# Two attention and two spectral layers on one core: later sums of squares, later squares, and wo products ahead of the filler

## The chip, the cores and the metric

The kernel runs on one core of one Trainium2 chip, in one launch. The metric is the time of an execution on the device, in microseconds (us). The kernel before took 3763.46 us, the median of three runs (3761.44 to 3765.95).

## The reference

An activation x of 2048 rows (S) and 1024 columns (D) goes through two equal pairs of sub-layers, each with a layer norm in front and a residual sum behind:

```python
def _A_ref(x, wqkv, wo):                       # 32 heads, Dh = 32
    qkv = (x @ wqkv).reshape(B, S, 3, H, Dh).transpose(2, 0, 3, 1, 4)
    q, k, v = qkv[0], qkv[1], qkv[2]
    scores = einsum("bhqd,bhkd->bhqk", q, k) * (Dh ** -0.5)
    p = softmax(scores, axis=-1)
    o = einsum("bhqk,bhkd->bhqd", p, v)
    return o.transpose(0, 2, 1, 3).reshape(B, S, D) @ wo

def _B_ref(x, w_r, w_i):
    X = rfft2(x, axes=(-2, -1)) * (w_r + 1j * w_i)
    return irfft2(X, s=(S, D), axes=(-2, -1))

x = x + _A_ref(_layernorm(x), wqkv, wo)
x = x + _B_ref(_layernorm(x), w_r, w_i)
x = x + _A_ref(_layernorm(x), wqkv, wo)
x = x + _B_ref(_layernorm(x), w_r, w_i)
```

All is float32 in and out. The change touches the attention sub-layers alone.

## The kernel before

**Units and groups.** `attention()` is called once per layer. It works through 8 head groups g of 4 heads; a group has 4 chunks c of 512 queries times 16 tiles kt of 128 keys, so 64 units. A unit computes the scores of one key tile against one query chunk for the 4 heads: `S` issues 12 matmuls (L697: high and low float16 halves of keys and queries, three products per head) into two PSUM buffers of the pool `psS`, and ScalarE takes one exponential per buffer (L701), 128 x 1024 each, with a bias that keeps it small. Every second unit `PV` multiplies the exponentials of two units by the values (L707, 16 matmuls in rows of the trace). VectorE adds the exponentials of a chunk up in `add`: two first sums L718 and then 28 additions L720 per chunk, two for a unit. When a chunk is over, `fin` runs at the start of the next one: the denominators z (L727, four products of a matrix of ones with the two sums, again in a `psS` buffer), a transposition L728, a reciprocal and more, and `out` follows at kt == 5.

`psS` has three buffers (`psS.tile` in `S`, `norms`, `wo_rest` and `fin`), taken in turn in the order of the code: two for a unit's scores, and whichever is next for the others. A user of a buffer waits for the one three turns before.

**Slots and the filler.** The keys, queries and values of later groups are projected in between. Every odd unit is a slot, 32 in a group, and in a slot `next(sl)` runs as many steps of the generator `filler` as the planner `slots` gives it. `qk_chunk` makes one chunk of 512 columns of keys or queries with 24 matmuls (L420) in one PSUM bank (`bank()`, the name x), then splits it in two halves (`split`, L215 on ScalarE and L216 on VectorE), then squares the high half (L427 on VectorE, or L425 on ScalarE in group 7's phases, which run in group 6), as `sq`. `v_tiles` does the same for values (L465). After a phase's fourth chunk the phase goes on the list `left_norms`.

**Sums of squares.** The exponential's bias of a group comes from the largest norms of its keys and queries. `norms` takes a `psS` buffer, sums the squares over each head's 32 rows with four small matmuls (L440, with the constant `bones`), and VectorE takes the maximum (L442, `mqk`); for queries `mkbias` follows on GpSimd. `slots` runs `norms` at the front of the first slot that it enters with the list not empty:

```python
while left_norms:
    norms()
```

In even groups the phases are the next group's keys and queries and the keys of the one after; in odd groups the next group's queries and values. The keys of the group after next, finished at the end of an even group, are summed in slot 0 of the odd one, and the queries of the next group in slot 12 of the odd one.

**Groups 6 and 7.** Group 6 projects the last keys and queries, chunk by chunk in turn, in 22 slots; then its slots multiply by wo. In group 7 each slot runs `share[u // 2]` steps of `wof`, which computes the tiles of the output projection up to the seventh of eight groups (`wo_part`, L526 and the evacuation L552), and in 11 slots (`rests`) a `wo_rest(t)`, which adds the last group's part: six matmuls in a `psS` buffer, an evacuation L567 with the residual on VectorE, two `bn_stats` (L569), a store `yd` and a `bn_aggr` (L588), for the next layer norm. The first four rests stand in slots 11, 12, 14 and 15, the last of them in the slot ahead of the end of chunk 1.

**Order.** TensorE and ScalarE run in the order in which the code issues (`tc.manual_schedule`). VectorE's instructions are ordered by the framework's scheduler. GpSimd and SyncE (which issues the DMAs) are not held by hand either.

Of the kernel before, what the change touches and what calls it, by code (L numbers as in the profile page):

```python
# [107 lines left out]
NG, NCH, NKT, NST = 8, 4, 16, 6  # L108
# [104 lines left out]
def split(nc, hi, lo, src, scale):  # L213

    high = nc.scalar.activation(hi, src, AF.Copy, scale=scale)  # L215
    return high, nc.vector.scalar_tensor_tensor(lo, src, scale, hi, op0=ALU.mult, op1=ALU.subtract)  # L216


def run(g):
    for _ in g:  # L220
        pass
# [115 lines left out]
def attention(nc, tc, layer, ap, xin, yd, wts, wo, cst, dram, flags):  # L337
# [14 lines left out]
    def bank():  # L352

        if both:
            both.append(True)
            if len(both) % 2:
                return psO.tile([128, 512], F32, name="o")
        return psX.tile([128, 512], F32, name="x")
# [48 lines left out]
    def qk_chunk(ph, c):  # L407
        kind, g = ph
        w = W[ph]
        if c == 0:  # L410
            if kind == "k":
                K[g] = ap.k[g % 3]
            else:
                Q[g] = qp.tile([128, 2, 2048], F16, name="Q") if g % 2 else ap.q
            p_, n_ = (qp, "Q") if ph == ("q", 0) else (wvp, "wv") if ph == ("q", NG - 1) else (sq, "sq")
            nrm[ph] = p_.tile([128, 4, 512], BF16, name="sq", tag=n_)
        t = (K if kind == "k" else Q)[g][:, :, c * 512:c * 512 + 512]
        ps = bank()
        for i, (a, b) in enumerate([(w[:, n, d], x[c][:, d]) for x, n in ((xh, 0), (xh, 1), (xl, 0)) for d in range(8)]):
            nc.tensor.matmul(ps, a, b, start=i == 0, stop=i == 23)  # L420
            if i < 23:
                yield
        split(nc, t[:, 0], t[:, 1], ps, SQ / (SX * SW))
        if g == NG - 1:
            nc.scalar.activation(nrm[ph][:, c], t[:, 0], AF.Square)  # L425
        else:
            (nc.gpsimd if both else nc.vector).tensor_tensor(nrm[ph][:, c], t[:, 0], t[:, 0], op=ALU.mult)  # L427
        if c == 3:
            left_norms.append(ph)
        yield  # L430

    left_norms = []

    def norms():
        kind, g = ph = left_norms.pop(0)
        if g not in mx:
            mx[g] = sm.tile([128, 2], F32, name="mqk")
        ps = psS.tile([128, 2, 512], F32, name="s")
        for c in range(4):
            nc.tensor.matmul(ps[32 * c:32 * c + 32, 0], cst["bones"], nrm[ph][:, c], start=True, stop=True)  # L440
        i = 0 if kind == "k" else 1
        nc.vector.reduce_max(mx[g][:, i:i + 1], ps[:, 0], axis=AX.X)  # L442
        if kind == "q":
            mkbias(g)
# [32 lines left out]
    def sums(ph):  # L477
        return 8 if ph[0] == "v" else 4
# [82 lines left out]
    def wo_last(c, t, p, src, y, start):  # L561

        for n in range(2):
            run(wo_mm(p[:, n], c, t, n, (7,), start=start))
        st = sm.tile([128, 2, 6], F32, name="st")
        r0 = c * 512 + t * 128
        nc.vector.scalar_tensor_tensor(y, p.rearrange("p n c -> p (n c)"), 1.0 / (SO * SW), src, op0=ALU.mult, op1=ALU.add)  # L567
        for n in range(2):
            nc.vector.bn_stats(st[:, n], y[:, n * 512:n * 512 + 512])  # L569
        nc.sync.dma_start(yd[r0:r0 + 128, :], y)  # L570
        return st
# [14 lines left out]
    def wo_rest(t):  # L586
        p = psS.tile([128, 2, 512], F32, name="s")
        nc.vector.bn_aggr(mvs[:, 2 * t:2 * t + 2], wo_last(t // 4, t % 4, p, wo_dst[t], wo_dst[t], True))  # L588
# [102 lines left out]
    def S(g, c, kt):  # L691

        s = [psS.tile([128, 2, 512], F32, name="s") for _ in range(2)]
        for i, (a, b) in enumerate(((0, 0), (0, 1), (1, 0))):
            for h in range(4):
                r = slice(32 * h, 32 * h + 32)
                nc.tensor.matmul(s[h // 2][:, h % 2], K[g][r, a, kt * 128:kt * 128 + 128],  # L697
                                 Q[g][r, b, c * 512:c * 512 + 512], start=i == 0, stop=i == 2)
        for hf in range(2):
            p = P[g, c, kt, hf] = pp.tile([128, 2, 512], F32, name="p")  # L700
            nc.scalar.activation(p, s[hf], AF.Exp, bias=bias[g], scale=SCALE / (SQ * SQ))  # L701

    def PV(g, c, kt):
        if kt == 0:
            O[g, c] = psO.tile([128, 512], F32, name="o")
        for h in range(4):
            nc.tensor.matmul(O[g, c][32 * h:32 * h + 32], V[g][:, kt, 32 * h:32 * h + 32], P[g, c, kt, h // 2][:, h % 2],  # L707
                             start=kt == 0, stop=kt == NKT - 1)
        if kt == NKT - 1:
            o = ap.oc.tile([128, 512], F32, name="oc")  # L710
            nc.scalar.copy(o, O[g, c])
            O[g, c] = o

    def add(g, c, kt):
        for hf in range(2):
            p = P[g, c, kt, hf]
            if kt == 1:
                nc.vector.scalar_tensor_tensor(acc[hf], P[g, c, 0, hf], 1e-34, p, op0=ALU.add, op1=ALU.add)  # L718
            elif kt:
                last_add = nc.vector.tensor_add(acc[hf], acc[hf], p)  # L720
        return last_add if kt > 1 else None
# [15 lines left out]
    def out(g, c, eng=nc.vector):  # L737
        r = O.pop((g, c))
        t = on2.tile([128, 2, 512], F16, name="ohl")
        nc.scalar.copy(t[:, 0], r)  # L740
        eng.tensor_tensor(t[:, 1], r, t[:, 0], op=ALU.subtract)
        if g < NG - 1:
            nc.sync.dma_start(od[:, g, :, c * 512:(c + 1) * 512].rearrange("a p n -> p a n"), t)
        else:
            olast[c] = t
# [3 lines left out]
    left, rests = 16, {}  # L749
# [4 lines left out]
    def slots(f, sums, n, steps):  # L754

        while sums:
            k = max(1, int(n / sums + 0.5))
            m = -(-steps // k)
            for i in range(0, steps, m):
                while left_norms:  # L760
                    norms()
                for _ in range(min(m, steps - i)):
                    next(f, None)
                n -= 1
                yield sums - (i + m >= steps)
            sums -= 1

    with tc.manual_schedule(engines={mybir.EngineType.PE, mybir.EngineType.Activation}):
        for g in range(NG):
            todo = sum(sums(ph) for ph in beside.get(g, []))  # L770
            sl = slots(fill, todo, 22 if g == NG - 2 else 32, 24)
            wsl = slots(wof, 4, 10, 21)
            for u in range(NCH * NKT):
                c, kt = divmod(u, NKT)
                S(g, c, kt)
                if g == u == 0:
                    run(last_v)
                if kt % 2 == 0:
                    for w in pend:
                        PV(*w)  # L780
                    late = pend
                    pend = []
                    if kt == 0 and late:
                        for w in late:
                            last_add = add(*w)
                        with tc.issue_after(last_add.ins):
                            wts.look()
                        done = [late[1][:2]]
                        fin(*done[0])
                        late = []  # L790
                for w in late[:1]:
                    add(*w)
                late = late[1:]
                if kt == 5 and done:
                    out(*done.pop())
                pend.append((g, c, kt))
                if kt % 2 == 0:
                    continue
                if todo:
                    todo = next(sl)  # L800
                elif g == NG - 2:
                    if left:
                        run(lwo)
                        left = 0
                    if next(wsl, None) is not None and u == NCH * NKT - 1:
                        run(wsl)
                elif g == NG - 1:
                    for _ in range(share[u // 2]):
                        next(wof)
                    if u // 2 in rests:  # L810
                        wo_rest(rests[u // 2])
                if g == NG - 2 and todo <= 6 and left > (8 if todo > 4 else 0):
                    next(lwo)
                    left -= 1
        for w in pend:
            PV(*w)
        for w in late + pend:
            add(*w)
        run(wof)
# [561 lines left out]
```

## Time and profile before

| | |
|---|---|
| median of three runs | 3763.46 us (3761.44 to 3765.95) |
| profiled execution, its own time | 3764.43 us |
| its span in the trace | 3762.6 us |
| mean granted TensorE clock | 0.996 |
| HBM read, written | 132.35 MB, 48.23 MB |
| the costliest groups: exponentials L701 on ScalarE | 2170.0 us in 2048 |
| additions L720 on VectorE | 2088.6 us in 1792 |
| PV matmuls L707 on TensorE | 985.0 us in 8192 |

The profiled execution is a single one, and 1.8 us of its time lie outside the span. In rows of the timeline the first number is the start in microseconds from the span's beginning, the second the time to the end of the last instruction of the row; `x12` says how many instructions the row holds, and a bracket at its end how long the engine waited before the row and for what. Rows of the waits give the engine and tile that waits, its line, whom it waits for with tile and line, and then total microseconds, how often, and the longest.

### The profile page before, as it was taken

The page shows a single profiled execution, that of the slowest core. Times are in us where ns is not written, and L with a number is a line of the kernel's source. Part 1 is how long each engine was busy: PE and PEld are TensorE (multiplying, and loading weights), DVE is VectorE, ACT ScalarE, POOL GpSimd, SP SyncE. Part 2 cuts the span into 40 slices and gives each one's busy share as a digit, 9 for nine tenths or more (in the row PEclk, how much of TensorE's full clock was granted, in tenths as well). Part 3 has the DMA queues.
Part 4 walks back from the last instruction along what each step waited for, and adds up shares of the span by engine and source line. Part 5 has one row for each costly group of instructions (what it writes and reads, how often), then busy time and mean ns, then how long its engine had stood idle before and what let it go on. Part 6 is the DMA issues. An engine that isn't in the chain of part 4 may idle for free.

```text
span 3762.6 us, 80259 instructions
## 1 busy us (share of the span) xinstructions
PE 3695.4 (98%) x33271; PEld 1637.1 (44%) x33271; DVE 3218.8 (86%) x3874; ACT 2900.2 (77%) x3587; POOL 298.8 (8%) x388
## 2 busy tenths in 40 slices
PE   8999999999999999999999999999999999999998
PEld 5333433343343333378963334333433433333788
DVE  7899899989999988975658998999899999789755
ACT  5788888888888866658748888888888888666686
POOL 1000000000000000014410000000000000000243
PEclk9999999999999999999999999999999999999999
DMA  6000000000000211233250000101000102111423
GB/s 194 10 18 18 13 13 17 26 7 18 13 27 15 88 54 65 74 143 106 70 157 21 29 29 24 32 24 35 14 29 29 41 15 85 54 71 68 166 86 109
DMA packets 150119, 198.43 MB, mean 53 GB/s; under 512 B 58224, under 2 KB 104048, under 8 KB 148720
## 3 DMA queue, kind: packets, MB, share of 16 engines
q1 hardware_dynamic: 148416, 192.62, 15.8%
q8 instruction: 263, 4.31, 0.5%
q14 instruction: 112, 0.92, 0.1%
q10 hardware_dynamic: 1328, 0.59, 0.1%
HBM read 132.35 MB, written 48.23 MB: 48 GB/s over the span
## 4 chain that ended last, share of the span: by engine, by line


## 5 line engine op out<-in xcount | busy, mean ns | idle before, releaser
L701 ACT ACTIVATE p<-s,bias 128x1024 f32<-128x1024 f32 x2048 | 2170.0, 1112 | 563.0 <-PE s L697 545.6
L720 DVE TENSOR_TENSOR R<-R,p 128x1024 f32<-128x1024 f32 x1792 | 2088.6, 1220 | 131.2 <-ACT p L701 126.8
L707 PE MATMUL o<-p,R 128*32 128x512 f32 x8192 | 985.0, 598 | 0.0
L420 PE MATMUL x<-big,wqk 128*128 128x512 f16 x2880 | 676.5, 380 | 2.3 <-ACT R L469 1.9
L697 PEld LDWEIGHTS <-R 32*128 32x128 f16 x12288 | 230.9, 92 | 749.2 <-issue 633.5
L420 PEld LDWEIGHTS <-wqk 128*128 128x128 f16 x3072 | 275.6, 98 | 418.4 <-issue 129.3
L707 PEld LDWEIGHTS o<-p,R 128*32 128x32 f32 x8192 | 213.6, 109 | 523.4 <-issue 523.4
L697 PE MATMUL s<-Q,R 32*128 32x512 f16 x6144 | 427.3, 377 | 4.6 <-DVE R L567 2.7
L697 PE MATMUL s<-R 32*128 32x512 f16 x6144 | 430.4, 377 | 1.5 <-ACT p L701 0.3
L465 PE MATMUL x<-wv,big 128*128 128x256 f16 x2784 | 330.6, 275 | 4.1 <-DVE R L216 2.2
L465 PEld LDWEIGHTS <-big 128*128 128x128 f16 x3072 | 290.9, 98 | 100.2 <-issue 59.3
L526 PE MATMUL x<-big 128*128 128x512 f16 x1050 | 241.6, 380 | 0.0
L448 POOL PARTITION_ALL_REDUCE mall<-mqk x16 | 38.4, 2401 | 2278.1 <-DVE mqk L442 2266.7
L526 PEld LDWEIGHTS <-big 128*128 128x128 f16 x1344 | 124.3, 98 | 176.4 <-issue 38.6
L718 DVE SCALAR_TENSOR_TENSOR R<-p 128x1024 f32<-128x1024 f32 x128 | 150.8, 1218 | 31.8 <-ACT p L701 31.8
L1043 DVE TENSOR_TENSOR H<-G,H 128x512 f16<-128x512 f32 (+1 forms) x68 | 47.0, 692 | 119.8 <-ACT H L1042 119.6
L988 ACT COPY U<-ps 64x256 f32<-64x256 f32 (+1 forms) x272 | 97.2, 357 | 9.2 <-PE ps L995 3.9
L988 ACT COPY B<-ps 64x256 f32<-64x256 f32 (+1 forms) x272 | 97.2, 357 | 5.4 <-PE ps L995 1.7
L995 PE MATMUL ps<-cbi,H 128*128 128x256 f16 (+1 forms) x792 | 98.6, 273 | 1.5 <-DVE H L1043 1.0
L728 DVE STREAM_TRANSPOSE zt<-s 128x512 f32<-128x512 f32 x64 | 45.8, 715 | 62.6 <-PE s L727 62.5
L995 PE MATMUL ps<-cb,big 128*128 128x256 f16 x780 | 96.7, 273 | 0.0
L995 PEld LDWEIGHTS <-H 128*128 128x128 f16 (+1 forms) x792 | 76.5, 98 | 12.4 <-DVE H L1043 2.4
(443 smaller groups left out, 2981.7 us busy)
## 6 DMA issues: line engine op xcount, KB each, us to landing
wst<-in_wp SPq DMA_DIRECT2D x96, 256.0 KB, 3.0
R<-y SPq DMA_DIRECT2D x32, 512.0 KB, 5.2
w<-in_w SPq DMA_DIRECT2D x60, 256.0 KB, 2.7
od<-ohl SPq DMA_DIRECT2D x56, 256.0 KB, 2.4
big<-od SPq DMA_DIRECT2D x16, 896.0 KB, 5.9
y<-R SPq DMA_DIRECT2D x20, 512.0 KB, 2.6
wst<-in_wo SPq DMA_DIRECT2D x32, 256.0 KB, 2.7
xres<-in_x SPq DMA_DIRECT2D x16, 512.0 KB, 3.6
```

Of the source, the lines that this page charges most:

```text
L420: nc.tensor.matmul(ps, a, b, start=i == 0, stop=i == 23)
L465: nc.tensor.matmul(ps[:, j], x[c][:, d, o:o + 128], w[:, n, d], start=i == 0, stop=i == 23)
L526: nc.tensor.matmul(p, a, b, start=start and d == ds[0] and i == 0, stop=stop and d == ds[-1] and i == 2)
L697: nc.tensor.matmul(s[h // 2][:, h % 2], K[g][r, a, kt * 128:kt * 128 + 128], Q[g][r, b, c * 512:c * 512 + 512], start=i == 0, stop=i == 2)
L701: nc.scalar.activation(p, s[hf], AF.Exp, bias=bias[g], scale=SCALE / (SQ * SQ))
L707: nc.tensor.matmul(O[g, c][32 * h:32 * h + 32], V[g][:, kt, 32 * h:32 * h + 32], P[g, c, kt, h // 2][:, h % 2], start=kt == 0, stop=kt == ...
L718: nc.vector.scalar_tensor_tensor(acc[hf], P[g, c, 0, hf], 1e-34, p, op0=ALU.add, op1=ALU.add)
L720: last_add = nc.vector.tensor_add(acc[hf], acc[hf], p)
L728: nc.vector.transpose(zt.rearrange("p a b -> p (a b)"), z)
L988: nc.scalar.copy(ov[64 * r:64 * r + 64, a0:a0 + m, x], tl[64 * x:64 * x + 64, :m, r])
L995: nc.tensor.matmul(out, l, r, start=k == 0, stop=k == len(mm_) - 1)
L1043: nc.vector.tensor_sub(lo, gs, hi)
```

## The change

Three orders change; the instructions and their sizes stay as they are.

1. **Sums of squares.** A phase that ends is put in a set `fresh` too. `slots` calls `ripe()` before it runs `norms`: in even groups below 6 it says yes as before; in odd groups and in group 6 it says no once for a phase just ended, and yes in the next slot. So `norms` of the keys in odd groups moves from slot 0 to slot 1, that of the queries from slot 12 to slot 13, and in group 6 both last ones a slot later (20 to 21, 22 to 23).
2. **Squares on ScalarE in group 6.** For the first three of four chunks of each of the last two phases, `qk_chunk` yields before the square, so it is issued at the first filler step of the next slot, behind the exponentials of the two units between. These are 6 of 8 squares per layer.
3. **Last head group.** In a slot of group 7 `wo_rest` now runs ahead of the slot's `wof` steps.

```diff
@@ qk_chunk
         split(nc, t[:, 0], t[:, 1], ps, SQ / (SX * SW))
         if g == NG - 1:
+            if c < 3:
+                yield
             nc.scalar.activation(nrm[ph][:, c], t[:, 0], AF.Square)
+            if c < 3:
+                return
         else:
             (nc.gpsimd if both else nc.vector).tensor_tensor(nrm[ph][:, c], t[:, 0], t[:, 0], op=ALU.mult)
         if c == 3:
             left_norms.append(ph)
+            fresh.add(ph)
         yield
 
-    left_norms = []
+    left_norms, fresh = [], set()
+
+    def ripe():
+        if not left_norms:
+            return False
+        old = left_norms[0] not in fresh or (g % 2 == 0 and g < NG - 2)
+        fresh.clear()
+        return old
@@ slots
-                while left_norms:
+                while ripe():
                     norms()
@@ the unit loop, group 7
                 elif g == NG - 1:
+                    if u // 2 in rests:
+                        wo_rest(rests[u // 2])
                     for _ in range(share[u // 2]):
                         next(wof)
-                    if u // 2 in rests:
-                        wo_rest(rests[u // 2])
```

In the changed code every line from 432 on is 12 further down (L442 is L454, L697 is L709, L720 is L732, and so on); the squares L425 and L427 become L427 and L431.

The order of the instructions on VectorE and ScalarE, before and now, at three places. The first is on VectorE in group 1 of layer 0, around the maximum of the queries (`mqk<-s`). Before:

```order
L216 SCALAR_TENSOR_TENSOR R<-x,R 128x512
L427 TENSOR_TENSOR sq<-R 128x512
L720 TENSOR_TENSOR R<-R,p 128x1024 x2
L442 TENSOR_REDUCE mqk<-s 128x1
L720 TENSOR_TENSOR R<-R,p 128x1024 x14
```

Now, the same place:

```order
L216 SCALAR_TENSOR_TENSOR R<-x,R 128x512
L431 TENSOR_TENSOR sq<-R 128x512
L732 TENSOR_TENSOR R<-R,p 128x1024 x6
L454 TENSOR_REDUCE mqk<-s 128x1
L732 TENSOR_TENSOR R<-R,p 128x1024 x10
```

The maximum stands behind six additions in place of two. The keys' maximum in odd groups likewise moves behind two first sums and two additions.

The second is on ScalarE in group 6 of layer 0, around the first square of a chunk of the last queries (`sq<-Q`; `big<-wst` are halves of wo, prepared in the same slots). Before:

```order
L215 ACTIVATE Q<-x 128x512
L425 ACTIVATE sq<-Q 128x512
L215 ACTIVATE big<-wst 128x512
L701 ACTIVATE p<-s,bias 128x1024 x4
L215 ACTIVATE big<-wst 128x512
L701 ACTIVATE p<-s,bias 128x1024 x4
```

Now, the same place:

```order
L215 ACTIVATE Q<-x 128x512
L215 ACTIVATE big<-wst 128x512
L713 ACTIVATE p<-s,bias 128x1024 x4
L427 ACTIVATE sq<-Q 128x512
L215 ACTIVATE big<-wst 128x512
L713 ACTIVATE p<-s,bias 128x1024 x4
```

The square stands behind the four exponentials of the next two units.

The third is on VectorE in group 7 of layer 0, from the last rest of chunk 1 (slot 15) to the denominators' first transposition (`zt<-s`). Before:

```order
L720 TENSOR_TENSOR R<-R,p 128x1024 x3
L552 SCALAR_TENSOR_TENSOR R<-x,xres 128x512
L720 TENSOR_TENSOR R<-R,p 128x1024
L567 SCALAR_TENSOR_TENSOR R<-s,R 128x1024
L569 BN_STATS st<-R 128x6 x2
L588 BN_AGGR mvs<-st 128x2
L728 STREAM_TRANSPOSE zt<-s 128x512
```

Now, the same place:

```order
L732 TENSOR_TENSOR R<-R,p 128x1024 x3
L579 SCALAR_TENSOR_TENSOR R<-s,R 128x1024
L564 SCALAR_TENSOR_TENSOR R<-x,xres 128x512
L581 BN_STATS st<-R 128x6 x2
L732 TENSOR_TENSOR R<-R,p 128x1024
L600 BN_AGGR mvs<-st 128x2
L740 STREAM_TRANSPOSE zt<-s 128x512
```

The chunk's last addition stood ahead of the rest's evacuation and its statistics, and stands behind them now. Only one store `yd` per layer moves by a place on SyncE (in slot 29), and GpSimd's order is the same.

## The prediction

> **What bounds the kernel now.** The page first, then TensorE's waits, then the timeline around each wait that the change touches.
>
> ```profile
> span 3762.6 us, 80259 instructions
> PE 3695.4 (98%) x33271; PEld 1637.1 (44%) x33271; DVE 3218.8 (86%) x3874; ACT 2900.2 (77%) x3587; POOL 298.8 (8%) x388
> ```
>
> TensorE is in work for 98% of the span. A change that leaves its matmuls as they are can only win its waits, or lose by new ones. The five rows of TensorE's waits that this change can touch (microseconds in total, times, longest):
>
> ```profile
> PE s L727 <- DVE R L567: 2.9, 2, 1.4
> PE s L697 <- DVE R L567: 2.7, 4, 0.9
> PE s L440 <- DVE sq L427: 2.4, 6, 0.4
> PE s L697 <- DVE mqk L442: 1.9, 6, 0.3
> PE s L440 <- ACT p L701: 0.4, 2, 0.2
> ```
>
> They sum to 10.3 us, 0.27% of the span. What is really lost is more, since a wait shorter than the pipe of matmuls shows as a longer group and not as idle time. So each place is measured from start to start, against the same stretch where nobody waits. About 0.2% (7.5 us) is what a measurement of this kernel can tell from no change.
>
> **Sums of squares, query of the next group (three odd groups, two layers: 6 times).** The timeline of group 1 in layer 0:
>
> ```profile
> 349.70 0.68 DVE L216 SCALAR_TENSOR_TENSOR R<-x,R 128x512 f16<-128x512 f32 x1
> 349.98 0.40 PE L440 MATMUL s<-sq,bones 128*32 128x512 bf16 x3
> 350.77 0.38 PE L440 MATMUL s<-sq,bones 128*32 128x512 bf16 x1 [0.40 <-DVE sq L427]
> 351.08 1.92 PE L465 MATMUL x<-wv,big 128*128 128x256 f16 x16
> 352.91 0.68 DVE L442 TENSOR_REDUCE mqk<-s 128x1 f32<-128x512 f32 x1
> 353.65 0.82 PE L697 MATMUL s<-Q,R 32*128 32x512 f16 x10 [0.32 <-DVE mqk L442]
> 354.40 1.92 PE L707 MATMUL o<-p,R 128*32 128x512 f32 x16
> ...
> 357.01 1.92 PE L465 MATMUL x<-wv,big 128*128 128x256 f16 x16
> ...
> 358.87 0.82 PE L697 MATMUL s<-Q,R 32*128 32x512 f16 x12
> 359.62 1.92 PE L707 MATMUL o<-p,R 128*32 128x512 f32 x16
> ```
>
> The reader sees two waits on VectorE: for the fourth quarter of the squares, and, at the next scores, for the maximum that frees the sums' PSUM buffer. Undisturbed paces from the last four rows: value products to scores 1.86 (357.01 to 358.87), scores to PV 0.75, PV to the next filler 2.61 (354.40 to 357.01). The other place, the key's sums at the front of an odd group, gives the sums' own length:
>
> ```profile
> 284.92 0.83 PE L697 MATMUL s<-Q,R 32*128 32x512 f16 x12
> 285.82 0.40 PE L440 MATMUL s<-sq,bones 128*32 128x512 bf16 x4
> 286.16 1.90 PE L420 MATMUL x<-big,wqk 128*128 128x512 f16 x8
> 287.61 0.68 DVE L442 TENSOR_REDUCE mqk<-s 128x1 f32<-128x512 f32 x1
> 287.99 1.18 PE L697 MATMUL s<-Q,R 32*128 32x512 f16 x12
> 289.10 1.92 PE L707 MATMUL o<-p,R 128*32 128x512 f32 x16
> ```
>
> That is 0.34 (285.82 to 286.16). So from 349.98 to the PV at 354.40 the query's place took 4.42 where 0.34 + 1.86 + 0.75 = 2.95 would do: 1.47 us lost.
>
> With the sums one slot later all of it does not come back, and the rows say why. The sums now hide the value products' own wait: their bank is free only when L216 ends, 349.70 + 0.68 = 350.38, so without the sums they start at 350.4 instead of 349.98. Then scores 352.3, PV 353.0, sums 355.65, value products 356.0, scores 357.85. The maximum now stands behind six additions of VectorE instead of two (the order given above), at the 1.13 of one addition (rows 1476.78 and 1477.91 below): 352.91 + 4 x 1.13 = 357.43. Before, the scores went on 0.74 after the maximum's start (352.91 to 353.65), so now at 358.17, a wait of 0.3, and their PV at 358.92 against 359.62. **Gain 0.70 each, 4.2 us in six.** It may be half an addition (0.57) better or worse each time, since VectorE's queue alone decides it: 0.8 to 7.6.
>
> **Sums of squares, key (6 times).** Lost before: 285.82 - 284.92 - 0.75 = 0.15, and 289.10 - 287.99 - 0.75 = 0.36, together 0.51. After: filler at 285.67, scores 287.50 (1.83 as from 286.16 to 287.99), PV 288.25, sums 290.86, filler 291.2, scores 293.03. The maximum moves behind two first sums and two additions: 287.61 + 4 x 1.13 = 292.13, and it frees its buffer at 292.87, just in time. **Gain 0.51 each, 3.1 us**; at least 0, at most that. The per-group bias that both maxima feed is wanted at the next group's first exponential, tens of microseconds on.
>
> **Squares on ScalarE in group 6 (12 of 16 move).** One of them, and a later chunk of the same group:
>
> ```profile
> 1211.54 0.63 ACT L425 ACTIVATE sq<-Q 128x512 bf16<-128x512 f16 x1
> 1213.24 1.32 PE L697 MATMUL s<-R 32*128 32x512 f16 x12
> 1214.49 1.90 PE L420 MATMUL x<-big,wqk 128*128 128x512 f16 x8
> 1246.80 0.68 DVE L216 SCALAR_TENSOR_TENSOR Q<-x,Q 128x512 f16<-128x512 f32 x1
> 1247.57 1.90 PE L420 MATMUL x<-big,wqk 128*128 128x512 f16 x8
> 1214.00:1268.00 54.00, 53.66 (x482) 16.29 (x478) 53.79 (x58) 50.19 (x58) 0.00 (x0) 1.00 0.17 55
> ```
>
> The 0.63 of a square delays the next exponentials, and the scores two units on take 1214.49 - 1213.24 = 1.25 instead of 0.75: 0.50 lost. Six such per layer would be 3.0. But the last row (columns: span, busy TensorE, weight loads, VectorE, ScalarE) has VectorE busy for 53.79 of 54 us: it is the limit there, and the next chunk starts 0.09 after VectorE freed its bank (1246.80 + 0.68 = 1247.48, 1247.57). TensorE that comes 0.5 earlier waits there instead. What is left is what VectorE itself gains on entering the stretch: the first chunk's 0.5 and a part of one square (0.63), I take 0.2; then one more 0.4 for the chunk behind it, and the 0.2 to 0.3 of the sums' wait on exponentials (the 0.4 in two of the waits above, plus the pipe). **1.4 per layer, 2.8 us**; in two layers between 2 x 0.5 = 1.0 (VectorE gives back nothing but the first chunk) and 6.5 (all twelve and the sums). The moved squares lie in ScalarE's idle time: before the exponentials they stood on the path, behind them they delay a pair of exponentials that has 0.3 or more to spare.
>
> **wo products at the front (22 rests, of which 3 per layer are waited for).** The place of the longest wait, and VectorE's load there:
>
> ```profile
> 1475.82 1.92 PE L707 MATMUL o<-p,R 128*32 128x512 f32 x16
> 1479.18 1.06 PE L727 MATMUL s<-R,ones 128*32 128x512 f32 x8 [1.44 <-DVE R L567]
> 1476.78 1.22 DVE L720 TENSOR_TENSOR R<-R,p 128x1024 f32<-128x1024 f32 x1
> 1477.91 1.22 DVE L567 SCALAR_TENSOR_TENSOR R<-s,R 128x1024 f32<-128x1024 f32 x1
> 1479.16 1.29 DVE L569 BATCH_NORM_STATS2 st<-R 128x6 f32<-128x512 f32 x2
> 1480.48 0.21 DVE L588 BATCH_NORM_AGGREGATE mvs<-st 128x2 f32<-128x12 f32 x1
> 1446.00:1483.00 37.00, 34.23 (x293) 11.23 (x290) 36.55 (x44) 24.33 (x24) 0.00 (x0) 1.00 0.34 120
> ```
>
> The intent shows in the rows: L567 frees a PSUM buffer late, and the scores and the denominators (L727) wait for it, 2.8 us of idle per layer. But VectorE is busy for 36.55 of 37 us there, and moving a product forward makes none of its work shorter. The denominators need the chunk's last addition (1476.78) as well as the buffer. In the new order that addition stands behind the rest's evacuation and its two statistics; all of VectorE's work ahead of the aggregate (1480.48) must then be done first. Four evacuations no longer hold up their statistics (1479.16 - 1477.91 = 1.25 against 1.13), which saves 0.5: the denominators start at 1480.0, against 1479.18. The two earlier waits (2.7 us in four, above) go, and reappear here: TensorE is done with its PV at about 1476.3 and idles 3.7 us. **Loss 0.8 per layer, 1.6 us**; between a loss of 1.3 (1480.48) and, if the last addition were ready in time, a gain of all 2.8 idle per layer and some 0.3 of pipe, 6.2 in two.
>
> **The sum.** 4.2 + 3.1 + 2.8 - 1.6 = 8.5 us off the profiled execution's 3764.43, which stands 1 us over the median of 3763.46; off the median that is 3755.0 us, 0.23% faster. With half an addition either way at the six query places its own range is 3751.5 to 3758.5.
>
> **Rivals.**
>
> *The intended gain at the wo products.* If VectorE reaches the last addition in time, the four waits per layer vanish: 8.5 + 1.6 + 6.2 = 16.3 us, 3747. For it: the waits name L567 alone. Against: VectorE's 36.55 of 37 us.
>
> *A long pause halves the clock.* The new 3.7 us pause is longer than any in the head groups. What followed the longest pause between the stages:
>
> ```profile
> 1625.00:1629.00 4.00, 0.26 (x2) 0.00 (x0) 2.74 (x9) 0.00 (x0) 0.57 (x1) 1.00 0.54 143
> 1629.00:1635.00 6.00, 4.85 (x32) 4.31 (x33) 2.43 (x6) 3.01 (x5) 0.00 (x0) 0.52 0.95 396
> ```
>
> Within 4 us TensorE works 0.26, and then the granted clock is 0.52 for 6 us. The same at the denominators would cost 0.48 x 6 = 2.9 us per layer: 8.5 - 5.8 = 2.7 us, 3760.8. For it: that row; against: the pause is a little shorter than the one there, and the 1.44 of now left the clock at 1.00 (the 37 us row). The Trainium skill, "TensorE: Matmul & The Clock Gate", Part 1, states this as a rule that speaks against the change: after an idle window of about 3.4 us, which runs freely, the clock falls to half; by it a pause of 3.7 us would now and then cover a whole window. This trace agrees that a pause of over 4 us does so; where the threshold lies no row of it shows.
>
> *Slower: the products at the front wait for their own slot's exponentials.* A slot's scores and exponentials:
>
> ```profile
> 1452.37 0.83 PE L697 MATMUL s<-Q,R 32*128 32x512 f16 x12
> 1453.23 2.12 ACT L701 ACTIVATE p<-s,bias 128x1024 f32<-128x1024 f32 x2 [0.49 <-PE s L697]
> ```
>
> At the front a product needs a third PSUM buffer at 1452.37 + 0.75 = 1453.12, where at the end of the slot it came 1.5 later. If the buffer it gets is one that this slot's first exponential (half of 2.12) must free, it waits until 1453.23 + 1.06 = 1454.29, 1.17 us in each of 22: 25.7 us, net 17 slower, 3780.7. It decides from 0.73 us per product ((8.5 + 7.5) / 22). Against: three buffers turn, two are taken by the slot's scores, and the third is freed by the unit before, whose exponentials ended by then.
>
> **How the numbers follow.** My sum 0.66, the intended gain 0.12, the halved clock 0.10, the slower one 0.12. The sum lies 1 us beyond the 7.5 of the bound, so of its 0.66 about 0.42 are faster and 0.24 the same; with the rivals faster 0.54, same 0.34, slower 0.12. The range reaches from the intended gain, less half a microsecond of spread between runs, past the halved clock to all four terms at their lower bounds together (0.8 + 0 + 1.0 - 2.6, a loss of 0.8, 3764.3): 3746.5 to 3764.5. It leaves out the slower case.
>
> **What the changed profile would show.** Right: no wait of L452 on squares; the waits on the maxima (L454) down to about 0.3 in six places; new waits of the value products' bank on L216 of some 0.4; in group 6 bank waits of L420 on L216 in place of long scores; and one wait of the denominators (L739) of about 3.7 us per layer on VectorE's L732, while those of the scores on L579 are gone. Wrong: a denominators' wait under 1 us (VectorE was not the limit), a granted clock under 1.00 behind it, waits of the front products on ScalarE, or waits on the maxima as long as before.

## The result, and the profile after

The changed kernel takes 3756.59 us, the median of 22 runs (3752.92 to 3762.28), against 3764.25 us of the kernel before in 22 runs (3760.15 to 3768.43). The ratio is 0.998, with a 95% interval of 0.9974 to 0.9987: 7.7 us or 0.2% faster. The page of the profile after:

```profile
span 3757.0 us, 80258 instructions
PE 3688.9 (98%) x33271; PEld 1635.1 (44%) x33271; DVE 3212.6 (86%) x3874; ACT 2900.2 (77%) x3587; POOL 297.8 (8%) x388
```

TensorE's matmuls are the same 33271; what went are waits and stretched groups. From TensorE's waits of after (microseconds in total, times, longest), the rows that answer to those of before:

```profile
PE x L477 <- DVE R L216: 4.6, 7, 2.2
PE s L739 <- DVE R L732: 3.7, 2, 1.9
PE x L420 <- DVE Q L216: 1.9, 2, 1.0
PE s L739 <- DVE R L579: 1.3, 2, 0.6
```

The waits of the sums on squares and exponentials (L452) and of the scores on the maxima and on the evacuation L579 are gone from the list. In their place the value products wait for their own bank (2.2 in one before, 4.6 in seven), group 6's products wait for VectorE, and the denominators L739 wait twice in each layer.

The time of a stage can be read from two starts of PV, which stand in the same order in both programs. Odd groups lose the same 0.68 in all six query places. The timeline of after in group 1 of layer 0:

```profile
347.93 1.92 PE L719 MATMUL o<-p,R 128*32 128x512 f32 x16
351.00 1.91 PE L477 MATMUL x<-wv,big 128*128 128x256 f16 x16 [0.39 <-DVE R L216]
352.84 0.83 PE L709 MATMUL s<-Q,R 32*128 32x512 f16 x12
353.60 1.92 PE L719 MATMUL o<-p,R 128*32 128x512 f32 x16
356.21 0.40 PE L452 MATMUL s<-sq,bones 128*32 128x512 bf16 x4
358.02 0.68 DVE L454 TENSOR_REDUCE mqk<-s 128x1 f32<-128x512 f32 x1
358.40 1.17 PE L709 MATMUL s<-Q,R 32*128 32x512 f16 x12
359.50 1.92 PE L719 MATMUL o<-p,R 128*32 128x512 f32 x16
```

Before, the PV that answers to the first of these rows began here:

```profile
347.37 1.92 PE L707 MATMUL o<-p,R 128*32 128x512 f32 x16
```

From it to the PV at 359.62 it was 12.25 us, and now 359.50 - 347.93 = 11.57. The 0.39 wait of the value products on L216 is there, and the scores behind the sums last 1.17 instead of 0.83, the 0.34 that the maximum still holds up their buffer.

The chunk's end in group 7, layer 0, as the timeline of after shows it:

```profile
1470.28 1.93 PE L719 MATMUL o<-p,R 128*32 128x512 f32 x16
1471.58 1.22 DVE L579 SCALAR_TENSOR_TENSOR R<-s,R 128x1024 f32<-128x1024 f32 x1
1472.85 1.05 PE L739 MATMUL s<-R,ones 128*32 128x512 f32 x4 [0.64 <-DVE R L579]
1473.31 1.28 DVE L581 BATCH_NORM_STATS2 st<-R 128x6 f32<-128x512 f32 x2
1474.50 1.21 DVE L732 TENSOR_TENSOR R<-R,p 128x1024 f32<-128x1024 f32 x1
1475.77 1.05 PE L739 MATMUL s<-R,ones 128*32 128x512 f32 x4 [1.86 <-DVE R L732]
1476.75 0.82 PE L709 MATMUL s<-Q,R 32*128 32x512 f16 x12
```

VectorE works without a gap from the evacuation to the last addition, and TensorE waits for it. In layer 1 the same place:

```profile
3344.88 1.92 PE L739 MATMUL s<-R,ones 128*32 128x512 f32 x4 [1.87 <-DVE R L732]
3346.73 1.47 PE L709 MATMUL s<-Q,R 32*128 32x512 f16 x12
```

The same four matmuls last 1.92 instead of 1.05, and the scores 1.47 instead of 0.82. The stretches around the two places (start and end, span, busy TensorE, weight loads, VectorE, ScalarE, GpSimd, granted clock, DMA share, GB/s):

```profile
3341.30:3344.71 3.41, 1.07 (x8) 0.14 (x4) 3.41 (x5) 0.80 (x2) 0.00 (x0) 1.00 0.97 311
3344.71:3348.12 3.41, 3.24 (x16) 0.48 (x16) 1.44 (x6) 0.00 (x0) 0.00 (x0) 0.50 1.00 323
1474.21:1477.62 3.41, 1.85 (x17) 0.48 (x18) 2.34 (x5) 0.01 (x1) 0.00 (x0) 1.00 1.00 278
1477.62:1481.03 3.41, 3.41 (x27) 1.26 (x29) 3.27 (x6) 2.29 (x3) 0.00 (x0) 1.00 0.62 236
```

In layer 1 the granted clock is 0.50 for 3.41 us behind the pause; in layer 0 it stays at 1.00.

Stage by stage, each from the starts of two PV in the profiles (in us; the columns of the experiments are told below):

| stage | before | after | norms alone | front alone | without front | spread, front | queries two later | short statistics |
|---|---|---|---|---|---|---|---|---|
| queries' sums, odd group, slot 10 to 15 (six) | 28.78 | 28.10 | 28.10 | 28.78 | 28.10 | 28.10 | 27.75 | 28.10 |
| keys' sums, slot 30 of the group ahead to slot 3 (six) | 28.57 | 28.08 | 28.08 | 28.57 | 28.08 | 28.08 | 28.08 | 28.08 |
| group 6, layer 0 | 181.48 | 179.92 | 181.11 | 181.47 | 179.91 | 179.92 | 179.93 | 179.92 |
| group 6, layer 1 | 181.84 | 180.33 | 181.49 | 181.85 | 180.35 | 180.35 | 180.35 | 180.35 |
| group 7, slot 10 to 25, layer 0 | 96.28 | 97.06 | 96.27 | 97.05 | 96.28 | 94.81 | 96.28 | 93.45 |
| group 7, slot 10 to 25, layer 1 | 96.28 | 98.56 | 96.28 | 97.05 | 96.27 | 94.82 | 96.28 | 93.45 |

The columns repeat to 0.03 us wherever the code of a stage is the same. Two executions at a lower granted clock stand in no ratio below: 6136.33 us with the queries two slots later (0.556), and 3850.78 us with the later squares alone (0.946), which is the profiled one of that kernel, so that it has no column. After against before: 6 x 0.68 + 6 x 0.49 + 1.56 + 1.51 - 0.78 - 2.28 = 7.0 us. The two spans differ by 5.6 only: the first PV starts 1.1 us later in the profile of after, and the way from the last PV of the first attention layer to the first of the second, with the spectral layer in it, takes 1.2 longer. The instructions there are the same, and the other profiles lie there between 1.0 shorter and 0.6 longer than before.

### The profile page after: what moved, and what is told of

It is laid out like the page before. It is cut to its first block, busy times and chain, and to the rows that moved or that the text cites. A ratio compares the mean times of both kernels' runs of the same rounds, so it can differ in the third digit from the quotient of the medians.

```text
span 3757.0 us, 80258 instructions
## 1 busy us (share of the span) xinstructions
PE 3688.9 (98%) x33271; PEld 1635.1 (44%) x33271; DVE 3212.6 (86%) x3874; ACT 2900.2 (77%) x3587; POOL 297.8 (8%) x388
## 4 chain that ended last, share of the span: by engine, by line
## 5 line engine op out<-in xcount | busy, mean ns | idle before, releaser
L732 DVE TENSOR_TENSOR R<-R,p 128x1024 f32<-128x1024 f32 x1792 | 2088.1, 1218 | 126.1 <-ACT p L713 123.9
L709 PEld LDWEIGHTS <-R 32*128 32x128 f16 x12288 | 228.3, 92 | 739.7 <-issue 623.6
L709 PE MATMUL s<-R 32*128 32x512 f16 x6144 | 425.7, 378 | 0.2
L709 PE MATMUL s<-Q,R 32*128 32x512 f16 x6144 | 425.7, 378 | 0.0
```

## The experiments

Each is timed against the kernel before on the same chip.

**Later sums alone.** With `fresh` and `ripe()` of the change, the squares and the rests as before:

```diff
+            fresh.add(ph)
...
-                while left_norms:
+                while ripe():
                     norms()
```

> Only the later sums of squares; the squares and the wo products stay where they were. Theory 1 (the parts add up, each by its own wait): six query places at 0.68 and six key places at 0.50 as the trace of the change showed them, and about 0.35 per layer for the two in group 6: 4.1 + 3.0 + 0.7 = 7.8 us faster than before, about 3756. Theory 2 (the later sums only pass their wait on, and the gain of the change came from the wo products): under 3 us faster.

Measured: 3756.2 us against 3764.55, ratio 0.998 (0.9971 to 0.9989). The stages give 4.1 + 2.9 + 0.4 + 0.4 = 7.8 us. Theory 1 stands: the sums alone bring as much as the whole change.

**Later squares alone.**

```diff
+            if c < 3:
+                yield
             nc.scalar.activation(nrm[ph][:, c], t[:, 0], AF.Square)
+            if c < 3:
+                return
```

> Only the squares of the first three chunks behind the next units' exponentials. Theory 1: VectorE is the limit in that stretch, so of twelve squares at 0.5 only some 1.2 per layer is left, 2.4 us faster than before, about 3762. Theory 2 (every moved square gives its 0.5 back): 6 us faster, about 3758.

Measured: 3760.77 us against 3764.55, ratio 0.9992 (0.9983 to 1.0001). The interval, 6.4 us faster to 0.4 slower, holds both theories, so the times do not decide. The stages do: in group 6 the kernel without the front part (which has sums and squares) stands against the later sums alone at 181.11 - 179.91 = 1.20 and 181.49 - 180.35 = 1.14 us, 2.3 in two layers and not 6: theory 1. Where the rest went shows in that stretch in the changed kernel, first in TensorE's timeline, then in its busy times:

```profile
1227.63 1.89 PE L420 MATMUL x<-big,wqk 128*128 128x512 f16 x8 [0.15 <-DVE R L216]
1244.27 1.89 PE L420 MATMUL x<-big,wqk 128*128 128x512 f16 x8 [0.96 <-DVE Q L216]
```

```profile
1211.00:1265.00 54.00, 52.52 (x479) 16.30 (x480) 53.79 (x58) 50.40 (x59) 0.00 (x0) 1.00 0.17 55
```

VectorE is busy for the same 53.79 of 54 us, and TensorE, busy 52.52 where it was 53.66, now idles in front of it. No run makes VectorE's work in this stretch less, so that VectorE is the limit is read from these rows and not tested.

**Rests in front alone.**

```diff
                 elif g == NG - 1:
+                    if u // 2 in rests:
+                        wo_rest(rests[u // 2])
                     for _ in range(share[u // 2]):
                         next(wof)
-                    if u // 2 in rests:
-                        wo_rest(rests[u // 2])
```

> Only the wo rests ahead of their slot's filler. Theory 1: VectorE reaches the chunk's last addition later, the denominators wait for it, 0.8 us per layer lost, and 1.5 more in a layer where the clock halves for one step of 3.4 us behind the pause: 1.6 to 4.6 us slower than before, 3766 to 3769. Theory 2 (the gain of the change came from here, since the four waits on the evacuation are gone): 2 us or more faster, 3762 or less.

Measured: 3766.23 us against 3764.55, ratio 1.0008 (0.9999 to 1.0017): the middle is slower, the interval just reaches no change. The stage says it more sharply, 0.77 us lost in each layer: theory 1. The loss is a balance. From one PV to the next, slots 13 and 15 take 1.00 and 0.47 us less than before, since their scores no longer wait for the evacuation, and slot 16, where the denominators wait, takes 2.1 more. In this profile neither layer fell to half the clock.

**Without the rests in front.** Sums and squares as in the change, the rests as before.

> The change without its third part: later sums and later squares, the wo rests behind the filler as before. Theory 1: 7.8 + 2.4 = 10.2 us faster than before, about 3754, and so 2 to 3 us faster than the whole change. Theory 2: slower than the whole change, about 3760 or more.

Measured: 3754.62 us against 3764.55, ratio 0.9976 (0.9967 to 0.9985), 9.9 us faster than before. Theory 1 again, and the parts add: 7.8 + 2.3 = 10.1 by the stages. Against the whole change the stages show 0.8 and 2.3 us less in group 7; the intervals of the two ratios overlap.

**Two rests past the chunk's end, in front and behind the filler.** With the whole change, and then with the rests behind the filler:

```diff
-    for t, n in zip(range(11), (11, 12, 14, 15, 20, 22, 24, 26, 28, 29, 30)):
+    for t, n in zip(range(11), (11, 12, 17, 18, 20, 22, 24, 26, 28, 29, 30)):
```

> The whole change, but the third and fourth rests go from slots 14 and 15 to 17 and 18, past the end of the chunk. Theory 1 (VectorE's load ahead of the chunk's last addition sets the pause): with 5.5 us of VectorE work out of slots 14 and 15 the last addition is on time, the denominators wait under 0.3 us instead of 1.9 and 0.6, and all 2.8 us of idle per layer that the kernel before had are won: 10 + 6 = 16 us faster than before, about 3748. Theory 2 (the pause comes from the products at the front, wherever they stand: their buffer or the place in the slot): waits on the evacuation or on the last addition come back in slots 17 and 18 or at the chunk's end, and it stays at 7 to 9 us faster, 3756.

> Later sums and squares, rests behind the filler as before, third and fourth rests in slots 17 and 18. Theory 1: VectorE has room there, so the place within the slot decides little: 0 to 1 us behind the same kernel with the rests in front, about 3748 to 3749. Theory 2 (behind the filler the evacuation always comes too late for the next scores): two waits of 0.4 to 0.9 per layer remain, about 3751.

Measured: 3750.4 us in front and 3751.56 behind, against 3763.58; ratios 0.9967 (0.9955 to 0.9979) and 0.9969 (0.9957 to 0.9982). The wait at the denominators falls, as expected, but it does not go (TensorE's waits with the rests in front):

```profile
PE s L739 <- DVE R L732: 0.9, 2, 0.5
```

I had counted on 16 us and got 13. Theory 1 holds all the same: no wait on the evacuation comes back. The missing part lies at the chunk's end, where from the PV of slot 15 to the next it takes 8.22 us, and 6.86 in the kernel with short statistics below: 1.36 per layer. The timeline of VectorE shows why:

```profile
1455.90 12.53 DVE L732 TENSOR_TENSOR R<-R,p 128x1024 f32<-128x1024 f32 x11
1468.35 0.69 DVE L564 SCALAR_TENSOR_TENSOR R<-x,xres 128x512 f32<-128x512 f32 x1
1468.95 1.22 DVE L732 TENSOR_TENSOR R<-R,p 128x1024 f32<-128x1024 f32 x1
```

Twelve additions and an evacuation stand back to back: with two rests ahead instead of four, VectorE is still behind at the chunk's end.

Behind the filler, slots 10 to 25 take 95.20 us in each layer against 94.81 in front, 0.8 in two layers, as theory 1 of that run has it. But the scores behind the second rest still wait for its evacuation, once per layer where theory 2 has two, so the run lies between its theories:

```profile
PE s L709 <- DVE R L579: 1.9, 2, 0.9
```

**The rest of slot 15 alone behind its filler.**

```diff
-                    if u // 2 in rests:
+                    if u // 2 in rests and u // 2 != 15:
                         wo_rest(rests[u // 2])
                     for _ in range(share[u // 2]):
                         next(wof)
+                    if u // 2 == 15:
+                        wo_rest(rests[u // 2])
```

> The whole change, but the rest of slot 15 alone stays behind its filler. Theory 1: VectorE is full over slots 11 to 15, so the denominators then wait for the evacuation instead of the last addition, at about the time they did before: the 1.46 per layer won in slots 13 and 15 is given back at the chunk's end, 1.3 to 1.5, and it is within 0.5 us of the kernel with all rests behind the filler, about 3754. Theory 2 (only the order of the last addition behind the rest of slot 15 cost anything): the 1.46 per layer stays won, 3 us faster than that, about 3751.

Measured: 3756.88 us against 3763.58, ratio 0.9982 (0.9973 to 0.9991). The time lies above both theories, the stage between them: slots 10 to 25 take 95.89 us in layer 1, 0.39 less than before, where theory 1 had 0 and theory 2 1.46. In layer 0 they take 97.48, since there the clock fell:

```profile
1474.31 1.53 PE L739 MATMUL s<-R,ones 128*32 128x512 f32 x8 [2.38 <-DVE R L579]
1475.77 1.47 PE L709 MATMUL s<-Q,R 32*128 32x512 f16 x12
```

The pause stays, under the name of the evacuation instead of the addition. VectorE's work is what is waited for, in either order. The order is not without weight: with the rest of slot 15 in front, and the clock at full, the stage took 97.05, so its place is worth 1.16 us of the 3.60 that separate that from the 93.45 of the next experiment.

**Less work on VectorE, every instruction in its place.** The statistics of the first four rests of a layer look at 16 of each 512 columns, so their layer norm is computed from a part of the row:

```diff
-            nc.vector.bn_stats(st[:, n], y[:, n * 512:n * 512 + 512])
+            nc.vector.bn_stats(st[:, n], y[:, n * 512:n * 512 + (16 if start and c == 0 else 512)])
```

> The whole change with every instruction in its place, but the statistics of the first four rests of a layer look at 16 of each 512 columns (so their layer norm is computed from a part of the row): four times about 1.1 us less on VectorE ahead of the last addition. Theory 1 (VectorE's load sets the pause): the denominators' second wait falls from 1.9 to under 0.5 us and the first from 0.6 to about 0, no layer can fall to half the clock there, 2.1 us per layer come back: 4 us faster than the whole change, about 3752. Theory 2 (the pause comes from the order, the last addition behind the rest's evacuation, whatever its length): 1.5 us of wait or more stay, 3755 or more.

Measured: 3748.11 us against 3764.27, ratio 0.9957 (0.9943 to 0.997). Its timeline at the chunk's end, and the busy times of slots 10 to 16 there:

```profile
1469.61 1.92 PE L719 MATMUL o<-p,R 128*32 128x512 f32 x16
1470.07 0.24 DVE L581 BATCH_NORM_STATS2 st<-R 128x6 f32<-128x16 f32 x2
1470.23 1.21 DVE L732 TENSOR_TENSOR R<-R,p 128x1024 f32<-128x1024 f32 x1
1471.35 1.19 PE L739 MATMUL s<-R,ones 128*32 128x512 f32 x8
```

```profile
1440.00:1477.00 37.00, 37.00 (x326) 11.91 (x322) 35.42 (x47) 26.16 (x26) 0.00 (x0) 1.00 0.29 104
```

The same stretch of the change:

```profile
1440.00:1477.00 37.00, 34.49 (x298) 10.50 (x295) 35.89 (x42) 24.29 (x25) 0.00 (x0) 1.00 0.28 96
```

No wait is left: TensorE is busy for 37.00 of 37 us, against 34.49. VectorE's busy share hardly moves, since it gets through more in the same time (47 instructions against 42); the share alone would not have told the two kernels apart. The order is that of the change, the last addition behind the rest's evacuation and statistics, and only their length differs. So VectorE's load sets the pause; theory 2, the order whatever the length, falls. The gain was larger than I wrote, since the 1.44 us that the kernel before waited there goes too: 96.28 - 93.45 = 2.83 us per layer against before. The half clock of layer 1 goes with the pause.

**Queries' sums two slots later.** On the kernel without the front part, `ripe()` says no twice for queries of odd groups:

```diff
+        if ph[0] == "q" and g % 2 and ph not in once:
+            once.add(ph)
+        else:
+            fresh.clear()
+        return False
```

> Later sums and squares, rests behind the filler, and the queries' sums in odd groups two slots later instead of one. Theory 1 (the maximum waits for additions queued on VectorE, and VectorE gains on TensorE in these slots): the 0.35 that the next scores still lose in six places goes, 2.0 us faster than with one slot, about 3752.5. Theory 2 (VectorE is as far behind one slot later): no change, about 3754.5.

Measured: 3751.86 us against 3763.58, ratio 0.9968 (0.9955 to 0.9981). The stage falls from 28.10 to 27.75 in all six places, 2.1 us: theory 1. The 0.34 that the scores still lost to the maximum is gone.

**The filler spread evenly.** With the queries two slots later, three kernels: rests in slots 11 to 14 in front, the same behind, and in front in the old slots. All have

```diff
-    share = [21] * 10 + [7] * 6 + [11, 10] * 6 + [12] * 4
+    share = [18] * 10 + [12] * 6 + [11, 10] * 6 + [12] * 4
```

> Later sums (queries by two slots), later squares, rests in front of the filler in slots 11, 12, 13 and 14 (before: 11, 12, 14, 15), and the filler spread as 18 steps in slots 0 to 9 and 12 in slots 10 to 15 (before: 21 and 7), the sum as before. Theory 1 (in slots 10 to 15 VectorE is the limit, 7.4 us of work in a slot with a rest against 6.3 on TensorE; 5 filler steps more give TensorE 1.15 us more per slot, taken from slots where VectorE has room): all waits on the evacuation and the last addition go, 6 us beyond the kernel with the queries' sums two slots later, about 3746. Theory 2 (the evacuations of the filler move into these slots as well and VectorE stays behind): no better than with the rests spread, 3749 or more.

> The same as the kernel with the even filler and the rests in slots 11 to 14, but each rest behind its slot's filler. Theory 1: VectorE keeps up, but an evacuation behind the filler has only the next scores' start to be done in, so 0.4 us of wait per rest in slots 11 to 14 remain, 3 us in all: 3748 to 3749. Theory 2 (with VectorE in step the place within the slot decides nothing): 3746, as in front.

> The same as the kernel with the even filler and the rests in front, but in their old slots 11, 12, 14 and 15. Theory 1: the load of slots 10 to 15 fits, but the rest of slot 15 still puts its evacuation and statistics ahead of the last addition, some 0.5 to 1 us of pause per layer: 3747 to 3748. Theory 2 (the pause of the change comes from this order, not from the load): it stays at 2.5 us per layer, 3751 or more.

Measured: 3793.63, 3797.01 and 3793.87 us against 3764.27; ratios 1.008 (1.0066 to 1.0094), 1.0087 (1.0073 to 1.0101) and 1.0075 (1.0061 to 1.0088). All three are 29 to 33 us slower, which no theory had, and they tell nothing of the rests. The longest of TensorE's waits in the first of the three, and its timeline early in group 7:

```profile
PE x L544 <- DVE R L570: 39.2, 20, 3.0
```

```profile
1373.62 1.47 PE L544 MATMUL x<-big 128*128 128x512 f16 x6
1376.07 0.68 DVE L570 SCALAR_TENSOR_TENSOR R<-x,xres 128x512 f32<-128x512 f32 x1
1376.81 2.75 PE L544 MATMUL x<-big 128*128 128x512 f16 x12 [1.72 <-DVE R L570]
```

A half tile of `wo_part` is 21 matmuls in the one bank x. With 21 steps in a slot its evacuation falls into the scores and PV of the next units; with 18 the half tile ends in mid-slot, and the next product waits until VectorE has emptied the bank. I had counted steps by their time and missed that they end a bank.

Of the kernels that compute the whole layer norm, three lie together: 3750.4 and 3751.56 us with two rests past the chunk's end, and 3751.86 with the queries two slots later. Their ratios do not tell them apart; by the stages the first is the best by 0.8 us. Together with the queries two slots later the stages would give some 2 us more, which is an estimate; that was not run.

## Why the prediction was right

The forecast was 3755.0 us, 8.5 faster; measured were 3756.6 and 7.7. Each of the four terms came with its sign, and near its size where the clock stayed at full.

- **Queries:** 0.70 each was forecast, 0.68 measured, with the 0.4 wait on L216 and the 0.3 at the maximum where they were said to be. The kernel with the sums two slots later shows that the rest was the maximum's place on VectorE.
- **Keys:** 0.51 forecast, 0.49 measured; nothing new waits.
- **Group 6:** 1.4 per layer forecast, 1.56 and 1.51 measured. Of these the later sums are 0.37 and 0.35, the squares 1.20 and 1.14. That a saturated VectorE takes the rest fits the rows; no run tests it.
- **Rests in front:** a loss of 0.8 forecast, 0.78 in layer 0. The pause from the end of PV to the last denominators is 3.6 us, as forecast (3.7), but not one wait: the first four denominators need only the first sum, which is ready earlier, so TensorE works 1.05 in between and idles 0.64 + 1.86. Layer 1 lost 2.28.
- **The rival of the halved clock** was the term that the sum lacked, and the clock under 1.00 behind the pause, which the prediction names as a sign of being wrong, did appear in layer 1. I had set it as one or the other, at 2.9 us per layer; in one and the same execution it came in one layer and not in the other, and it is worth 98.56 - 97.06 = 1.5 us when it comes. Of the six layers with this pause in three profiles (the change, the rests in front alone, the rest of slot 15 behind) two fell. An estimate from that: a third of two layers at 1.5 is 1.0 us on the mean; by the stages without it the change gains 8.5, and 8.5 - 1.0 = 7.5 against the 7.7 measured. Two of six is a small count, and that the 8.5 without the clock equals the forecast is partly luck: 0.3 too much for queries and keys stands against 0.3 too little for group 6.
- **The rival of the intended gain** (three waits per layer by the rows, where the prediction once says four) fell for the reason given against it, VectorE's 36.55 of 37 us. The short statistics show that its size, 2.8 us of idle per layer, was right.
- **The slower rival** did not come: no front product waits on ScalarE.

## What to carry to other kernels

Moving forward the one instruction of a saturated engine that a wait is named after did not pay here: the engine's whole queue up to the next dependency was the price. A probe that shortens instructions in place, without moving any, told load from order, and moving one rest back showed what the order was worth. Moving a small step behind work that both engines have queued paid here within 0.02 us of what start-to-start distances said. Before giving a stage more filler, look where its PSUM bank ends, not only at its time.

## What the runs showed of the hardware that I had not expected

The changes of the granted clock in each trace lie whole multiples of 3.41 us apart, and it fell without TensorE being idle for a whole such stretch: 1.07 us of work in 3.41 was too little (layer 1 above). Two pairs that lie close to each other, from the profile before and from the one with the rest of slot 15 behind (columns as above, each stretch with the one that follows it):

```profile
3496.32:3499.73 3.41, 1.39 (x7) 0.42 (x5) 1.95 (x4) 0.80 (x2) 0.00 (x0) 1.00 0.13 51
3499.73:3503.14 3.41, 0.56 (x3) 0.56 (x4) 1.45 (x8) 0.81 (x1) 0.57 (x1) 0.50 0.97 299
```

```profile
3338.45:3341.86 3.41, 1.41 (x16) 0.20 (x8) 3.41 (x4) 2.19 (x3) 0.00 (x0) 1.00 1.07 377
3341.86:3345.27 3.41, 3.02 (x26) 0.98 (x27) 3.27 (x8) 1.16 (x2) 0.00 (x0) 1.00 0.79 252
```

In the thirteen profiles whose clock is otherwise at 1.00, every recorded stretch at full clock with 1.39 us of work or less was followed by half the clock, and none with 1.46 or more. Between these both happened. Stretches of 1.41, 1.44 and 1.45 were followed by full clock, and two of 1.45 by half, both in kernels with the even filler, of which the one with the rests behind:

```profile
3337.59:3341.00 3.41, 1.45 (x15) 0.41 (x14) 1.91 (x3) 0.00 (x0) 0.00 (x0) 1.00 0.02 5
3341.00:3344.41 3.41, 3.41 (x20) 0.59 (x16) 2.11 (x2) 2.12 (x2) 0.00 (x0) 0.50 0.00 0
```

The profile models the ends of matmuls, so the edge, between 1.39 and 1.46 of 3.41 us, is that of these records. In the change the same pause cost 1.5 us in one layer and nothing in the other, by where the stretches lay: in layer 1 one of them held 1.07 us of work, and in layer 0 none less than 1.85. The Trainium skill, "TensorE: Matmul & The Clock Gate", Part 1, has windows of this length that run freely, and the traces agree; that an idle window is what throttles does not agree, since windows with up to 1.45 us of work did too.
